# A two-weight FFT mixer: one product instruction a unit, negated weights on VectorE, odd row pair 6 in cosine and sine parts, and a new order list

## The chip, the cores and the metric

The kernel runs on one core of one Trainium2 chip. TensorE (PE) multiplies matrices into PSUM, VectorE (DVE) and ScalarE (ACT) read PSUM and SBUF, GpSimd (POOL) works on SBUF alone, and SyncE (SP) issues nearly all DMAs. The metric is the device time of one execution in microseconds. Three runs of the kernel before took 115.3, 115.53 and 116.19 us; the median, 115.53 us, is what the prediction is set against.

## The reference

`x` is 2048 x 1024 in bf16. Both branches A and B take the real 2-D FFT of the same `x`, multiply it by a complex weight of 2048 x 513, and transform back. A gate, one number for each row, mixes the two results.

```python
def ref(x, w_r, w_i):                       # A and B alike
    X = jnp.fft.rfft2(x.astype(jnp.float32), axes=(-2, -1))
    X = X * (w_r + 1j * w_i)
    return jnp.fft.irfft2(X, s=(S, D), axes=(-2, -1)).astype(jnp.bfloat16)

x = A_x
g = _sigmoid((x * gate_w).sum(-1, keepdims=True))
a = _A_ref(x, A_w_r, A_w_i)
b = _B_ref(x, B_w_r, B_w_i)
return g * a + (1 - g) * b
```

## The kernel before

**Transform by matrices.** The row index of 2048 is split as 128 x 16 and the column index is folded into four quarters, so that the whole transform becomes products with fixed cosine and sine matrices. Even and odd column frequencies are two halves of the work ("parity" 0 and 1). There are 16 units of rows, `n`: units 0 to 7 belong to parity 0, units 8 to 15 to parity 1.

**The order list.** The whole program is written as a list of short tokens in the string `ORDER` (lines 24 to 66). Each token calls one small function (table `fn`, line 665), in the order of the list. Every engine executes its own instructions strictly in that order, so the list is also the queue of each engine; buffers and PSUM banks come in rings, and an instruction waits until the earlier readers of its buffer are done. A letter names the engine that does a copy: A for ACT, D for DVE, P for POOL. The last figures of a PE token are PSUM banks. For instance `R:10:1:D` copies half 1 of unit 10 from PSUM on VectorE, and `J:10:0:6` computes unit 10 into banks 0, 1 and 6, 7.

The tokens in the order of the data:

- `x`, `c`, `W` load the input (nine DMAs), the constants and the 16 units of weights, all on SP. A unit of weights is 512 KB. Units 0 to 7 lie in the tile `ro`, 8 to 11 in `wx`, 12 to 15 in a part of `y` that has to be read out first.
- `F1` (line 331) multiplies one of 16 input slices with the first Fourier matrix, for the even (`e`) or odd (`o`) columns. `FC` copies one half of the result from PSUM, `FD` (two instructions, line 379) adds and subtracts it on DVE. For eight of the odd slices `FX` copies all of it on ACT and `FP` adds and subtracts on POOL.
- `neg` (line 278) writes minus the imaginary part of a constant, in two pieces of 128x256 and 128x768, into the tile `wn`.
- `F2` and `F3` (lines 455, 485) are the next two transforms of a unit; `T` and `X` copy their results from PSUM. There are two `T` and two `X` buffers.
- `P` (line 505, function `prod`) multiplies a unit's spectrum `X` with its weights on DVE. `P:n:0` and `P:n:1` do it in two instructions of 128x2048, for the real and the imaginary part of `X`. `P:n:b` does both in one instruction with broadcast operands. There are three `p` buffers. `Y`, `NA`, `N` repair one column of units 0 to 7.
- `J` (line 548, 32 matmuls in small tiles) starts the way back, `R` copies it from PSUM into `rl`, two halves a unit, and `H` stores each half (256 KB) to a scratch tensor in DRAM. The ring of `rl` has five buffers, which the output tiles use later too.
- `L:parity:v` loads one of eight row pairs `v` (512 KB) back from the scratch tensor with rows and columns exchanged. Parity 0 goes into `re`, parity 1 into `ro`. Loads of a parity wait for all 16 stores of it.
- `V` (line 576) applies the last transform over rows with the gate weights (`GH` to `GB` compute these), `VC` copies it, 8 matmuls of 128x128 each.
- The last transform over columns stands in two forms. `U` (line 592) does four matmuls of 128x512 which give the sum and the difference of the cosine and sine parts in PSUM. `C` (line 601) does four of 128x256 which give the two parts side by side; somebody then has to add and subtract them.
- For parity 0 all row pairs use `C`. `EX` copies the parts and two `EQ` combine them (DVE or POOL, line 626), or `ES` and `EF` do, or `E` copies the parts as they are.
- For parity 1, `OR` (line 646) adds or subtracts the even and the odd result on DVE straight from PSUM; `OC` and `OP` (line 642) do the same through an ACT copy and POOL. Row pair 3 goes another way: its even part is only copied (`E`), its odd part comes from `C`, `QD` (line 653) adds and subtracts the parts in fp32 on DVE, and `QP` (line 658) combines them on POOL.
- `S` stores a row pair to the output (512 KB, or 256 KB for a half).

**What sets the order around the change.** In DVE's queue the folds `FD` come first, then the 32 products with the small repairs, some `R`, `T`, `VC` copies and the gate weights `GA`, `GB` between them, then the even outputs and at last the odd ones.

Of the kernel before, what the change touches and what calls it, by code (L numbers as in the profile page):

```python
# [10 lines left out]
P = 128  # L11
S = 2048
D = 1024
# [11 lines left out]
warm:8 c:A:F1 x:S:0:1 x:S:1:1 c:A:gws x:S:2:2 tab:A F1:0:e:4 x:S:4:2 FC:0:e:D F1:1:e:7 F1:0:o:5 x:S:6:2 FC:1:e:A FD:0:e  # L25
FX:0:o:A F1:1:o:0 FD:1:e F1:2:e:6 x:S:8:2 FC:2:e:D FX:1:o:A F1:3:e:2 FD:2:e FC:3:e:A FD:3:e FP:1:o FP:0:o x:S:10:2 x:S:12:2
F1:2:o:4 F1:3:o:7 F1:4:e:0 F1:5:e:6 x:S:14:2 FX:2:o:A FP:2:o FC:4:e:D c:S:w0 c:S:WF:0:4 c:S:PM c:S:WF:4:16 c:S:EZ c:S:FD:0:1
W:S:0 W:S:1 c:S:E c:S:WJ:0:4 c:S:WJ:4:16 F1:7:e:1 FC:5:e:A W:S:2 FX:3:o:A FD:4:e FD:5:e FP:3:o F1:6:e:3 FC:7:e:A F1:5:o:4
F1:9:e:0 F1:8:e:6 F1:7:o:5 FC:6:e:A FX:5:o:A FC:9:e:A FD:7:e FD:6:e FC:8:e:A F1:11:e:1 gc:P F1:10:e:7 FX:7:o:A F1:4:o:4
F1:12:e:3 F1:13:e:2 FC:11:e:A FC:10:e:A FP:5:o FD:9:e FD:8:e FD:11:e FX:4:o:A F1:9:o:1 F1:15:e:6 F1:14:e:0 F1:11:o:5 FP:7:o  # L30
FC:12:e:A FC:13:e:A neg:A:0:4 FC:15:e:A FD:10:e FP:4:o FD:12:e FC:9:o:A F1:13:o:7 FC:14:e:A FD:13:e F1:12:o:4 F1:6:o:2
FD:15:e FD:14:e FD:9:o F2:1:0:6 FC:11:o:A neg:A:4:16 FC:13:o:A FX:6:o:A F2:1:1:3 T:1:0:A FD:13:o FC:12:o:A F1:15:o:2 T:1:1:A
FC:15:o:A FD:11:o F1:14:o:1 F1:10:o:0 F3:1:6 F2:0:0:3 F1:8:o:5 FD:12:o FC:10:o:A F2:0:1:4 FC:14:o:A FD:15:o FD:10:o F2:2:0:2
FD:14:o X:1:A FC:8:o:A T:0:0:A pw:P T:0:1:A T:2:0:A FD:8:o F2:3:0:0 F2:2:1:7 T:2:1:A F3:0:5 X:0:A P:1:1 P:1:0 P:0:1 F2:3:1:4
Y:1:3 F2:4:0:7 T:3:1:A FP:6:o F3:2:1 NA:1:D Y:0:5 W:S:9 NA:0:D W:S:3 W:S:7 P:0:0 W:S:8 W:S:11 N:1:D W:S:6 W:S:4 c:S:FD:1:2
W:S:5 c:S:IG T:4:0:A GH:6 X:2:A T:3:0:A GC:A Y:2:4 NA:2:D F2:5:1:1 P:2:0 P:2:1 W:S:10 F3:3:2 T:5:1:A F2:4:1:4 N:0:D GT:2:5
J:1:6:0 GT:0:5 X:3:A GT:1:5 GT:3:5 T:4:1:A F3:4:3 R:1:0:A F2:5:0:2 R:1:1:D X:4:A T:5:0:A GK:D J:0:6:0 F2:6:0:4 P:3:1 F2:6:1:5
Y:3:3 R:0:0:A F3:5:6 R:0:1:A P:3:0 NA:3:D GZ:0:2 F2:7:0:0 X:5:A F2:7:1:1 W:S:14 T:6:1:D T:6:0:D N:3:D N:2:D GS:0 P:4:0
T:7:0:D J:3:4:6 W:S:12 W:S:13 W:S:15 T:7:1:A GZ:1:0 R:3:1:A R:3:0:D J:2:6:2 Y:5:4 P:4:1 GS:1 Y:4:5 NA:5:D NA:4:D P:5:0 P:5:1
R:2:0:A N:4:D F3:7:0 R:2:1:A X:7:A F2:8:1:5 F3:6:6 F2:8:0:4 T:8:0:A T:8:1:D J:4:2:0 F3:8:4 H:0:0 H:1:0 X:6:A R:4:1:A Y:7:7  # L40
P:7:1 F2:9:0:6 N:5:D R:4:0:A Y:6:0 P:7:0 H:1:1 X:8:A NA:6:D T:9:0:A H:0:1 NA:7:D GA:D:4 F2:10:1:1 H:2:0 H:3:0 H:3:1 F2:9:1:0
P:6:0 T:9:1:A N:7:D P:6:1 T:10:1:A J:5:2:4 J:7:0:6 R:5:1:A R:5:0:A F2:10:0:5 H:4:0 F3:9:2 F2:11:0:4 P:8:1 H:2:1 R:7:0:A N:6:D
R:7:1:D J:6:0:6 GB:D:4 H:4:1 T:10:0:A X:9:A H:7:0 H:5:0 P:8:0 T:11:0:D R:6:0:A GA:D:0 R:6:1:A F2:11:1:2 F3:10:3 P:9:0 H:5:1
P:9:1 H:7:1 H:6:1 X:10:A H:6:0 J:8:0:6 T:11:1:A R:8:0:D R:8:1:A F2:12:0:4 H:8:0 T:12:0:A P:10:1 P:10:0 F3:11:2 F2:12:1:5
# [679 lines left out]
```

## Time and profile before

| what | value |
|---|---|
| median of three runs | 115.53 us |
| time of the profiled execution | 116.1 us |
| its span, first to last instruction | 114.3 us |
| granted TensorE clock, mean | 0.991 |
| PE busy | 103.0 us (90%) |
| DVE busy | 100.9 us (88%) |
| ACT busy | 86.4 us (76%) |
| POOL busy | 39.5 us (35%) |
| moved by DMA | 36.79 MB, 322 GB/s over the span |

The busy time of PE is that of pipelined matmuls whose ends are modelled. A row of the groups gives the line of the code, the engine, the operation, what it writes and reads, its shapes and count, and then the busy time together, the mean of one instruction in ns, and the idle time before it with what ended it. A row of the timeline gives start and length in us and how many instructions are merged in it; consecutive instructions of one engine overlap a little, so that two of 1.218 us can take 2.36 us together. In the chain of waits a row gives start, length and what was being waited for.

### The profile page before, as it was taken

The page shows a single profiled execution, that of the slowest core. Times are in us where ns is not written, and L with a number is a line of the kernel's source. Part 1 is how long each engine was busy: PE and PEld are TensorE (multiplying, and loading weights), DVE is VectorE, ACT ScalarE, POOL GpSimd, SP SyncE. Part 2 cuts the span into 40 slices and gives each one's busy share as a digit, 9 for nine tenths or more (in the row PEclk, how much of TensorE's full clock was granted, in tenths as well). Part 3 has the DMA queues.
Part 4 walks back from the last instruction along what each step waited for, and adds up shares of the span by engine and source line. Part 5 has one row for each costly group of instructions (what it writes and reads, how often), then busy time and mean ns, then how long its engine had stood idle before and what let it go on. Part 6 is the DMA issues. An engine that isn't in the chain of part 4 may idle for free.

```text
span 114.3 us, 3946 instructions
## 1 busy us (share of the span) xinstructions
PE 103.0 (90%) x1616; PEld 70.3 (61%) x1619; DVE 100.9 (88%) x175; ACT 86.4 (76%) x140; POOL 39.5 (35%) x61
## 2 busy tenths in 40 slices
PE   5969999999999988989898989998999999999930
PEld 2569999875546543534453547845998966566510
DVE  0068999999998999999999999999999598998990
ACT  4054989999799899999999999999689762325400
POOL 1019999800000000000000000830382999997300
PEclk9999999999999999999999999999999999999996
DMA  3999999999999899997969999996999998099655
GB/s 75 330 331 406 405 374 318 350 338 376 398 406 416 257 361 281 376 377 245 339 232 262 393 391 301 369 386 228 335 281 351 377 390 345 3 377 398 271 222 199
DMA packets 17794, 36.79 MB, mean 322 GB/s; under 512 B 1904, under 2 KB 10736, under 8 KB 17776
## 3 DMA queue, kind: packets, MB, share of 16 engines
q1 hardware_dynamic: 17488, 36.44, 88.4%
q8 instruction: 12, 0.20, 0.6%
q10 hardware_dynamic: 288, 0.10, 0.6%
q14 instruction: 6, 0.05, 0.1%
HBM read 23.96 MB, written 12.58 MB: 320 GB/s over the span
## 4 chain that ended last, share of the span: by engine, by line
PE 18%; DMA 10%; ACT 9%; DVE 6%; issue 3%; SPq 3%; DVEq 1%; ACTq 0%
PE ps L592 7%; DMA ro<-sc 7%; PE ps L576 5%; ACT rl L201 4%; DVE p L505 3%; PE ps L548 3%; DMA sc<-rl 3%; DVE ot L646 3%; SPq L565 3%; ACT T L201 2%; ACT X L201 1%; PE ps L485 1%; PE ps L455 1%; ACT V L201 1%; PE ps L601 1%
## 5 line engine op out<-in xcount | busy, mean ns | idle before, releaser
L626 POOL TENSOR_TENSOR re<-wx 128x256 f32<-128x256 f32 x15 | 12.9, 883 | 58.7 <-ACT wx L201 50.0
L201 ACT COPY wx<-ps 128x256 f32<-128x256 f32 (+1 forms) x41 | 18.0, 467 | 12.3 <-PE ps L592 5.7
L201 ACT CAST rl<-ps 128x1024 bf16<-128x1024 f32 x25 | 24.6, 1042 | 0.7 <-PE ps L548 0.7
L548 PE MATMUL ps<-p,wj 32*64 32x512 bf16 x512 | 19.6, 380 | 2.6 <-ACT rl L201 1.4
L505 DVE TENSOR_TENSOR p<-X,ro 128x2048 bf16<-128x2048 bf16 x16 | 19.1, 1218 | 0.0
L455 PE MATMUL ps<-fd,y 128*128 128x256 bf16 x128 | 17.7, 273 | 0.4 <-ACT rl L201 0.2
L201 ACT CAST V<-ps 128x512 bf16<-128x512 f32 x23 | 13.0, 593 | 6.3 <-PE ps L576 4.8
L201 ACT CAST X<-ps 128x1024 bf16<-128x1024 f32 x16 | 16.7, 1044 | 0.2 <-PE ps L485 0.2
L331 PE MATMUL ps<-f,re 128*128 128x128 bf16 x256 | 15.9, 225 | 0.9 <-DMA re<-in_x_dram 0.9
L331 PEld LDWEIGHTS <-re 128*128 128x128 bf16 x256 | 15.4, 101 | 1.9 <-DMA re<-in_x_dram 1.4
L379 DVE TENSOR_TENSOR y<-ps,wx 128x256 bf16<-128x256 f32 x48 | 16.3, 416 | 0.1
L201 ACT CAST T<-ps 128x512 bf16<-128x512 f32 x26 | 15.2, 628 | 0.8 <-PE ps L485 0.8
L646 DVE TENSOR_TENSOR ot<-re,ps 128x512 bf16<-128x512 f32 x22 | 13.9, 683 | 0.9 <-PE ps L592 0.5
L548 PEld LDWEIGHTS <-wj 32*64 32x64 bf16 x512 | 8.2, 103 | 10.4 <-issue 6.8
L455 PEld LDWEIGHTS <-y 128*128 128x128 bf16 x128 | 11.1, 97 | 5.0 <-issue 3.8
L379 POOL TENSOR_TENSOR y<-wx 128x256 bf16<-128x256 f32 x16 | 11.1, 731 | 7.3 <-ACT wx L201 7.3
L592 PE MATMUL ps<-ig,V 128*128 128x512 bf16 x53 | 13.2, 379 | 0.2
L485 PE MATMUL ps<-T,wf 64*64 64x512 bf16 (+1 forms) x128 | 10.4, 334 | 0.6 <-ACT T L201 0.3
L505 DVE TENSOR_TENSOR p<-X,y 128x2048 bf16<-128x2048 bf16 x8 | 9.9, 1282 | 0.0
L601 PE MATMUL ps<-ig,V 128*128 128x256 bf16 x72 | 9.8, 273 | 0.0
L505 DVE TENSOR_TENSOR p<-X,wx 128x2048 bf16<-128x2048 bf16 x8 | 9.5, 1218 | 0.0
L203 DVE COPY wx<-ps 128x256 f32<-128x256 f32 (+1 forms) x8 | 4.2, 549 | 5.9 <-PE ps L331 5.9
(61 smaller groups left out, 144.3 us busy)
## 6 DMA issues: line engine op xcount, KB each, us to landing
sc<-rl SPq DMA_DIRECT2D x32, 256.0 KB, 5.5
ro<-in_we_dram SPq DMA_DIRECT2D x8, 512.0 KB, 6.9
re<-sc SPq DMA_DIRECT2D x8, 512.0 KB, 7.1
ro<-sc SPq DMA_DIRECT2D x8, 512.0 KB, 6.3
re<-in_x_dram SPq DMA_DIRECT2D x7, 512.0 KB, 9.0
out_dram<-ot SPq DMA_DIRECT2D x7, 512.0 KB, 2.7
wx<-in_wo_dram SPq DMA_DIRECT2D x4, 512.0 KB, 7.2
y<-in_wo_dram SPq DMA_DIRECT2D x4, 512.0 KB, 6.6
```

What stands on the lines that cost most here:

```text
L201: nc.scalar.copy(out=out, in_=in_)
L331: nc.tensor.matmul(o, lhsT=lh, rhs=rh, start=(h == 0), stop=(h == 1))
L379: Q[e].tensor_tensor(yo[:, v, k:k + n, s1, :], a.rearrange("p (k c) -> p k c", c=4), b.rearrange("p (k c) -> p k c", c=4), op)
L455: nc.tensor.matmul(ps[:, v * 256:v * 256 + 256], lhsT=y[:, v, par, b, 2 * t:2 * t + 2, :, :].rearrange("p j s c -> p (j s c)"), rhs=C["FD" ...
L485: nc.tensor.matmul(view(ps[ho, tt * 512:(tt + 1) * 512], dst), lhsT=lh, rhs=view(T[hp(jh), tt, :], src), start=(w == 0), stop=(w == 1))
L505: nc.vector.tensor_tensor(p[:, int(r)], xb, w, ALU.mult)
L548: nc.tensor.matmul(o, lhsT=lh, rhs=src[r, ri, wi, tt], start=(q == 0), stop=(q == 3))
L576: nc.tensor.matmul(ps[:, ch * 128:ch * 128 + 128], lhsT=RR[par][:, v, ch // 2, s, c0 + 256 * ab:c0 + 256 * ab + 128], rhs=Ew[:, s1, :], st ...
L592: nc.tensor.matmul(ps, lhsT=Vs[par, v][:, s, ch, :], rhs=rh, start=(ch == 0), stop=(ch == 3))
L601: nc.tensor.matmul(ps[:, o:o + 256], lhsT=Vs[par, v][:, s, ch, :], rhs=g[:, o:o + 256], start=(ch % 2 == 0), stop=(ch % 2 == 1))
L626: Q[e].tensor_tensor(EV[:, v, s, 256 * h:256 * h + 256], t[:, 0], t[:, 1], (ALU.add, ALU.subtract)[h])
L646: nc.vector.tensor_tensor(otile(v)[:, s, h, :], EV[:, v, s], PS["O", 1, v, s], (ALU.add, ALU.subtract)[h])
```

## The change

Four things change, all of them in the order list; no function is altered.

1. The 32 tokens `P:n:0` and `P:n:1` become 16 tokens `P:n:b`.
2. `neg:A:0:4` and `neg:A:4:16` become `neg:D:0:4` and `neg:D:4:16`.
3. Row pair 6 is done as row pair 3: `U:1:6:s` becomes `C:1:6:s`, the even part is copied by `E:6:s` instead of `EX:6:s` and four `EQ:6`, and four `OR:6` become four `QD:6` on DVE and four `QP:6` on POOL.
4. The list is ordered anew throughout, with other engines for some copies and other PSUM banks.

Copies that change engine, counted over the whole list: `R` on DVE from 7 to 8, `VC` on DVE from 9 to 5, `FC` on DVE from 3 to 2, `EX` on DVE from 4 to 2 and `E` on DVE from 0 to 2; `EQ` on POOL from 15 to 11, on DVE 5 in both; `T` on DVE 6 in both.

The core of the diff, the stretches that the prediction speaks of:

```diff
-FX:0:o:A F1:1:o:0 FD:1:e F1:2:e:6 x:S:8:2 FC:2:e:D FX:1:o:A F1:3:e:2 FD:2:e FC:3:e:A FD:3:e FP:1:o FP:0:o x:S:10:2 x:S:12:2
...
-FC:12:e:A FC:13:e:A neg:A:0:4 FC:15:e:A FD:10:e FP:4:o FD:12:e FC:9:o:A F1:13:o:7 FC:14:e:A FD:13:e F1:12:o:4 F1:6:o:2
...
-P:15:0 P:15:1 GA:D:8 J:13:4:2 EX:0:1:A VC:0:2:0:A VC:0:2:1:A J:14:0:6 R:13:0:A R:13:1:A J:15:4:2 GB:D:8 R:14:0:D EQ:0:1:1:D
-GA:D:12 H:13:0 R:14:1:A R:15:0:A GB:D:12 R:15:1:A H:14:1 H:14:0 H:13:1 C:0:1:0:6 H:15:0 H:15:1 L:0:5 L:1:3 L:1:1 V:0:4:1:7
...
-U:1:6:1:6 V:1:7:0:4 U:1:6:0:0 VC:1:7:0:A OR:7:1:1 OR:7:1:0 OR:6:1:0 U:1:7:0:4 OR:6:1:1 OR:6:0:1 OR:6:0:0 OR:7:0:1 OR:7:0:0
-S:S:7:1 S:S:6 S:S:7:0
+warm:8 c:A:F1 x:S:0:1 x:S:1:1 c:A:gws x:S:2:2 F1:0:o:1 F1:1:o:4 F1:0:e:2 FC:0:e:D F1:1:e:3 tab:A FX:0:o:A FX:1:o:A x:S:4:2
+x:S:6:2 x:S:8:2 F1:3:e:6 F1:2:e:1 FP:0:o c:S:EZ x:S:10:2 FC:3:e:A c:S:w0 c:S:E x:S:12:2 x:S:14:2 gc:P FP:1:o FC:1:e:D FD:1:e
...
+F2:1:1:2 F2:0:0:3 neg:D:4:16 FD:10:o FD:15:o neg:D:0:4 FD:12:o T:1:0:A FP:5:o F1:14:o:7 T:1:1:A F2:0:1:5 F1:11:o:6 FD:8:o
...
+R:6:1:A GA:D:8 R:6:0:D H:5:1 H:4:0 H:7:1 H:7:0 H:6:0 H:6:1 W:S:13 F2:12:0:3 X:10:A F2:11:1:7 F2:12:1:0 T:11:0:A W:S:12
...
+L:0:6 L:0:7 L:0:4 L:0:5 V:0:0:1:2 F2:15:1:3 R:10:0:A F3:14:0 R:10:1:A VC:0:0:1:A J:11:4:6 X:14:A F2:15:0:0 R:11:1:A C:0:0:1:1
+H:8:1 P:12:b H:8:0 H:9:1 H:9:0 H:10:0 H:10:1 V:0:0:0:6 R:11:0:A T:15:1:D GB:D:4 T:15:0:D P:14:b F3:13:2 V:0:1:1:7 EX:0:1:A
...
+EX:2:1:D GB:D:12 EQ:2:1:0:D R:13:1:D VC:0:1:0:A C:0:2:0:5 EX:2:0:A H:12:1 H:12:0 J:15:0:6 H:11:0 H:11:1 R:15:1:A V:0:6:0:4
+V:0:6:1:5 H:14:0 R:15:0:A H:14:1 C:0:1:0:3 H:13:0 H:13:1 GB:D:8 EX:1:0:A VC:0:6:0:A EQ:1:1:1:D EQ:2:0:0:D H:15:1 V:0:4:1:6
...
+VC:1:4:1:D S:S:3 U:1:7:0:4 U:1:4:0:3 U:1:7:1:5 U:1:4:1:7 OR:7:0:0 OR:7:0:1 OC:4:0:A S:S:0 S:S:5 S:S:2 EQ:7:1:1:P OR:7:1:0
+OR:7:1:1 OR:4:1:0 OR:4:1:1 S:S:6 S:S:7:0 OP:4:0:1 OP:4:0:0 S:S:7:1 S:S:4
```

65 lines of the change are left out of this document (30 added, 35 removed).

## The prediction

> **What bounds the kernel now.** I read the slices of the page first, to see which engine is ever free, then the stretches, then the chain of waits.
>
> ```profile
> span 114.3 us, 3946 instructions
> ...
> PE   5969999999999988989898989998999999999930
> ...
> DVE  0068999999998999999999999999999598998990
> ACT  4054989999799899999999999999689762325400
> ```
>
> PE and DVE are full from the fourth slice to the end, ACT to about 80 us; only the ends and the last third of ACT have room. The stretches say which engine has no slack in which part (columns: busy us and instructions of PE, weight loads, DVE, ACT, POOL; clock; DMA share; GB/s).
>
> ```profile
> 11.20:24.40 13.20, 13.20 (x213) 12.29 (x211) 13.16 (x41) 12.50 (x31) 10.97 (x27) 1.00 1.00 357
> 24.40:77.70 53.30, 49.20 (x968) 28.11 (x967) 52.31 (x69) 51.53 (x71) 3.25 (x2) 1.00 0.97 343
> 88.40:109.70 21.30, 20.99 (x197) 13.87 (x198) 19.06 (x34) 9.34 (x18) 17.79 (x18) 1.00 0.80 313
> ```
>
> From 11.2 to 24.4 us DVE does the folds, without a hole (13.16 of 13.20). From 24.4 to 77.7 us, first to last product, it is busy 52.31 of 53.30: its instruction list sets the pace. From 88.4 us on it is PE, 20.99 of 21.30. What lies between the last product and 88.4 is in the chain of waits, with the tail after it:
>
> ```profile
> 77.83 0.90 PE ps L548 x24
> ...
> 78.75 1.93 ACT rl L201 x2
> ...
> 81.04 3.23 DMA sc<-rl
> ...
> 95.54 0.62 PE ps L576 x8
> 96.16 2.59 PE ps L592 x12
> 98.75 0.45 PE ps L576 x8
> ...
> 107.56 2.54 DVE ot L646 x4
> ```
>
> ```profile
> L576 PEld LDWEIGHTS <-ro x72: 95/98/98, 88.6 to 95.9; 128*128 128x128 bf16 x72
> L565 SPq DMA_DIRECT2D ro<-sc x8: 332/434/1352, 84.5 to 88.6; - x8
> ...
> DMA to landing us min/median/max: 4.0/6.3/10.1
> ```
>
> The last unit's matmuls end at 78.73, its two copies at 80.68, the last store is issued at 81.04 and lands 3.23 us later; the eight loads of parity 1 start at 84.5, the quickest takes 4.0 us, so 88.5, and PE's first use of `ro` is at 88.6. From there PE's work decides (V, U, C), then DVE's last `OR`, then the last output store. So the time is: folds, DVE's product stage, a fixed trip through DRAM, PE's odd stage, a tail.
>
> **The change, part by part.** The sum is made against the profiled span of 114.3 us, whose execution took 116.1 us; that execution is 0.57 us above the median of 115.53, so I add the difference to the median. I counted tokens of DVE's queue in both lists.
>
> ```profile
> L505 DVE TENSOR_TENSOR p<-X,ro 128x2048 bf16<-128x2048 bf16 x16 | 19.1, 1218 | 0.0
> L203 DVE CAST rl<-ps 128x1024 bf16<-128x1024 f32 x7 | 8.5, 1221 | 0.3
> L203 DVE CAST V<-ps 128x512 bf16<-128x512 f32 x9 | 6.1, 682 | 0.2 <-PE ps L601 0.2
> L442 DVE TENSOR_TENSOR ea<-ea,e 128x512 bf16<-128x512 bf16 x4 | 1.7, 416 | 0.0
> L278 ACT ACTIVATE wn<-wf 128x768 bf16<-128x768 bf16 x1 | 0.9, 857 | 0.0
> ...
> 29.70 2.36 DVE L505 TENSOR_TENSOR p<-X,ro 128x2048 bf16<-128x2048 bf16 x2
> ...
> 70.67 4.02 DVE L505 TENSOR_TENSOR p<-X,y 128x2048 bf16<-128x2048 bf16 x3
> 72.02 3.25 POOL L626 TENSOR_TENSOR re<-wx 128x256 f32<-128x256 f32 x2 [49.69 <-ACT wx L201]
> ```
>
> *Products.* Two of 1.218 us take 2.36 us together: the second starts 1.14 us after the first, so about 0.08 us of each is hidden by its neighbour. A line through 128x512 (0.416) and 128x2048 (1.218) has a slope of 0.522 ns an element and 0.149 us fixed. One instruction of 4096 elements is then 2.29 us, against 2.36: 0.07 us saved a unit, 1.1 us in 16. Ends: nothing saved, and the whole fixed part, 16 x 0.149 = 2.4. I take 1.1, as the pair of row 29.70 shows it directly. [...]
>
> *Negations.* DVE has no such row before. The same line gives 0.55 us for 768 elements and 0.28 for 256; less 0.08 overlap each, +0.67 us. Bounds 0.2 (two very short DVE instructions) and 0.83 (no overlap). I keep 0.67, since the 128x512 row is near. They stand before the last folds, so all products move. ACT loses 0.857 us and its smaller piece, which buys nothing while DVE sets the pace. [...]
>
> *Start of the folds.* DVE's rows around the first input DMAs:
>
> ```profile
> 9.00 0.42 DVE L203 COPY wx<-ps 128x256 f32<-128x256 f32 x1 [1.33 <-PE ps L331]
> 9.46 1.42 DVE L379 TENSOR_TENSOR y<-ps,wx 128x256 bf16<-128x256 f32 x4
> ...
> 11.24 13.01 DVE L379 TENSOR_TENSOR y<-ps,wx 128x256 bf16<-128x256 f32 x39
> ```
>
> The new list does the odd groups of slices 0 and 1 first, so the first even copy comes two PE groups later. But before, DVE stands idle 1.33 us ahead of 9.00 us, until the third input DMA has fed PE. The late start falls into that hole, and the removed copy on DVE (0.42) is work taken from the same place, so 20 folds of 0.667 (13.01 x 2 / 39) remain from about 11.2 us in both. The three small constants now ahead of the last two input DMAs, and copies that ACT takes over, come late by my reading at slices 14 and 15: +0.2 us (0 to 0.5).
>
> *Product stage.* Between the first and last product DVE gets one `R` more (+1.14, row of 1221 less overlap), two `GA` more (2 x 0.41 = +0.82) and two `VC` fewer (2 x 0.60 = -1.20). `T`, `NA`, `N`, `GB` are as many as before. With the products: -0.34. Before, one product ran beside two POOL additions: rows 70.67 and 72.02 show three products in 4.02 us instead of 3.50, and two additions in 3.25. In the new list one POOL addition (`EQ:0:1:0`) falls into the stage, so I leave that loss of 0.5 us as it is. The last product then ends 0.67 + 0.2 - 0.34 = +0.53 us later.
>
> *Last product to first odd load.* The last two products before:
>
> ```profile
> 75.21 2.35 DVE L505 TENSOR_TENSOR p<-X,y 128x2048 bf16<-128x2048 bf16 x2
> ```
>
> `J:15` now uses bank 0, which holds `C:0:2:1` until DVE's `EX:2:1` has copied it, and that stands behind the last product: 0.60 (a copy of 128x512 like `VC`), then some 1.2 us of matmuls and 1.93 of copies. Before, the last copy ended 3.1 us after the last product (80.68 against 77.56) and SP issued 0.36 later, being busy with the other stores; the new order frees it. Sum 3.7 + 0.05 against 3.48: +0.27. The trip itself stays: one load of parity 0 precedes the odd ones in both lists.
>
> *Odd stage on PE.* Two `U` become two `C`.
>
> ```profile
> 103.98 0.86 PE ps L592 x4
> ...
> 71.76 0.44 PE ps L601 x4
> ```
>
> 2 x (0.86 - 0.44) = -0.84. PE begins with row pairs 1, 3, 6, 0 in the order of their loads, as before with 3, 1, 0; I see no new wait.
>
> *Tail.* DVE has as many instructions for odd rows as before (22 `OR` + 4 `QD` against 18 + 8). POOL gains 4 `QP` and loses 4 `EQ`.
>
> ```profile
> 104.94 6.35 DVE L646 TENSOR_TENSOR ot<-re,ps 128x512 bf16<-128x512 f32 x10 [0.35 <-issue]
> 107.75 1.89 PE L592 MATMUL ps<-ig,V 128*128 128x512 bf16 x8
> 100.58 2.50 POOL L642 TENSOR_TENSOR ot<-re,wx 128x512 bf16<-128x512 f32 x2
> 103.03 0.73 POOL L626 TENSOR_TENSOR re<-wx 128x256 f32<-128x256 f32 x1
> ...
> out_dram<-ot SPq DMA_DIRECT2D x7, 512.0 KB, 2.7
> ...
> out_dram<-ot SPq DMA_DIRECT2D x2, 256.0 KB, 2.4
> ```
>
> Now DVE ends 111.29 - 109.64 = 1.65 us after PE. In the new list POOL does 6 `OP` + 8 `QP` of 1.25 and `EQ:7:1:1` of 0.73 from the first odd `OC` on, 18.2 us. PE reaches that after three `V` (0.45), a `C` and a `U`, 2.65 us into the odd stage; with a copy of 0.6 POOL begins at 3.3 and ends at 21.5, and `OR:7:1` waits for `EQ:7:1:1` at 19.0. Four `OR` of 0.63 follow: 21.5. PE ends at 21.0 - 0.84 = 20.2, so DVE and POOL end at least 1.3 us after it; since POOL will hardly run without a hole I take 1.85, +0.2 (bounds -0.3 and +0.5). The last store is 512 KB instead of 256 KB: +0.3.
>
> **Sum:** +0.53 + 0.27 - 0.84 + 0.2 + 0.3 = **+0.46 us**, span 114.8, and 115.53 + 0.46 = **116.0 us**.
>
> **The rivals.**
>
> *A, faster.* The merged products save the whole fixed part (2.4 instead of 1.1) and the negations cost 0.2 instead of 0.67: 1.3 + 0.47 = 1.8 less, **114.2 us**. For it: the rows of short instructions do show a fixed part of 0.149. Against it: the pair of 2.36 us. [...]
>
> *B, slower: the stores wait behind the loads.* SP before, around the loads of parity 0 (`re<-sc`):
>
> ```profile
> 60.54 3.47 SPq L565 DMA_DIRECT2D re<-sc x7
> 64.45 17.04 SPq L560 DMA_DIRECT2D sc<-rl x14
> ```
>
> In the new list seven loads of parity 0 stand ahead of all stores of units 8 to 12 on SP, and two weight loads ahead of those; before, unit 8's stores and all weights had gone. Two stores and two weight loads are 1.5 MB at the 343 GB/s of the stretch: 4.4 us more in front of unit 11's stores. The copy of unit 15 needs unit 10's buffer, that of unit 14 unit 8's. By my count these land about 2 us ahead; the weight loads fit into the hole while the first load of parity 0 waits for its stores. If that hole is not there, up to 4.4 - 2 = 2.4 us come onto the path: **117.9 us** with half of it to all, 117.2 to 118.4.
>
> *C, slower: the product stage gets holes.* A product of 2.29 us gives nothing to `J` until it is done, and releases `X` and lets the next `R` on DVE start later; ACT (51.53 of 53.30) and PE (49.20) have so little slack that a hole of 0.15 us for each of 16 units gives +2.4: **118.4 us**. Against: `J` needs both halves already now.
>
> *D:* the broadcast over four dimensions falls to a lower rate; at the rate of the PSUM copies (0.682 us for 512 elements, less 0.149 fixed) a product would take 4.4 us, 16 x 2.0 more than a pair: **148 us**. `X` is read with a broadcast dimension in the rows before already, so there is hardly a chance.
>
> **How the numbers follow.** About 1% is what a measurement of this kernel can tell from no change. The forecast, within 1% (114.4 to 116.7): 0.43. A: 0.22. B: 0.19, C: 0.14, D: 0.02; together 0.35 slower. The unknown costs (products -1.3 to +1.1, negations -0.5 to +0.2, tail -0.5 to +0.5) span 114.3 to 117.3; the range reaches to A and B and into C, **113.9 to 118.2**.
>
> **What would show it.** Products of 2.25 to 2.35 us each in the groups, the last ending near 78.1; negations of 0.3 and 0.55; first use of `ro` near 89.4; 48 `U` matmuls instead of 56 and 80 `C` instead of 72; from there to PE's end 20.2 us; POOL nearly gapless in its last 18 us. It would be wrong if DVE has more than 1 us of holes in the product stage (C), if `R` on ACT waits for a landing store near 75 us (B), or if the first product starts later than 25.6 us.

## The result, and the profile after

The changed kernel takes **115.08 us** (median of 20 runs, 114.09 to 117.04) beside 115.91 us of the kernel before (20 runs, 115.14 to 117.14), 0.83 us less. The ratio is **0.9893**, 95% interval 0.9866 to 0.9921; here and below a ratio leaves out the slow runs, those more than 1.5% above the fastest of their kernel (the medians are then 114.65 and 115.89 us), while a median is that of all runs. So the change is worth about 1%, which is small but clear of the noise. I had forecast 116.0 us and 0.46 us slower; the time lies in my range, on the other side of no change. Single runs scatter by 2 to 3 us in both kernels, so each experiment below is compared with the runs of the kernel before that belong to it.

The profiled execution after has a span of 113.6 us and took 115.38 us. From its page, the slices of the span:

```profile
span 113.6 us, 3933 instructions
...
PE   5999979999988879798998989979999699999910
...
DVE  0079989999998999999999999999559849999870
ACT  4267848999989999999999999999976565635200
```

The stretches of after (columns as in the prediction: PE, weight loads, DVE, ACT, POOL, clock, DMA share, GB/s), from the first to the last product, from there to the first odd `V`, and from there to PE's end:

```profile
24.40:76.10 51.70, 46.35 (x947) 28.15 (x945) 51.12 (x54) 50.43 (x69) 2.50 (x1) 1.00 0.94 337
76.10:87.40 11.30, 11.19 (x165) 9.41 (x165) 8.64 (x18) 9.75 (x19) 4.88 (x7) 1.00 0.85 283
87.40:107.80 20.40, 19.37 (x192) 13.52 (x196) 17.74 (x32) 10.18 (x19) 17.24 (x16) 1.00 0.77 300
```

The product stage is 51.6 us long where it was 53.05, and DVE is still full in it. Between the stages PE is full (11.19 of 11.30), and in the odd stage PE now has a full us without work. The chain of waits of after, around the last store and the first odd loads (start, length, what was waited for):

```profile
66.73 8.73 DMA sc<-rl
75.46 0.03 ACTq L200
75.49 0.66 ACT rl L200
...
76.19 0.61 PE ps L575 x8
76.79 0.44 PE ps L600 x4
77.23 1.05 PE ps L547 x32
...
79.21 1.03 ACT rl L200
...
80.25 3.42 DMA sc<-rl
83.67 0.02 issue
...
84.26 5.43 DMA ro<-sc
89.69 0.05 issue
89.74 0.28 PE ps L575 x2
```

The chain goes through the landing of a store at 75.46, which ended a wait in ACT's queue ahead of a copy `R`, and of the last store at 83.67 (84.28 before), and then not through the first odd load but through the second, which PE gets at 89.7. The groups and the timeline show the parts of the change:

```profile
L501 DVE TENSOR_TENSOR p<-X,ro 128x4096 bf16<-128x4096 bf16 x8 | 18.1, 2279 | 0.0
```

```profile
19.73 0.66 DVE L279 TENSOR_SCALAR wn<-wf 128x768 bf16<-128x768 bf16 x1
...
21.64 0.21 DVE L279 TENSOR_SCALAR wn<-wf 128x256 bf16<-128x256 bf16 x1
...
24.43 2.27 DVE L501 TENSOR_TENSOR p<-X,ro 128x4096 bf16<-128x4096 bf16 x1
```

A product is 2.28 us, the negations are 0.66 and 0.21 us, and the first product starts at 24.43 us, where it started at 24.51 before.

The numbers of this table are used below for every kernel. They are taken from the same trace records as the views (landings from the completions of the DMAs). "Last load ahead" is the last of the loads of parity 0 that stand in front of the closing row of stores on SP; the number in brackets is how many stores land after it. "PE's end" is the end of PE's last weight load, in every kernel 0.49 us ahead of the end of its last matmul, which the prediction used (109.64 before, 108.30 after).

```
kernel                    last product  last store  last load   last store  from load to   first odd  PE's
                          ends          issued      ahead lands lands       store (stores) V          end
before                    77.56         81.05       74.08       84.28       10.20 (14)     88.56      109.15
before, second profile    78.24         81.72       75.34       85.12        9.78 (14)     89.24      110.15
after                     76.03         80.26       72.71       83.67       10.96 (16)     87.36      107.81
after, second profile     76.23         80.35       72.59       83.57       10.98 (16)     87.39      108.66
merge in before           79.44         82.93       75.59       86.29       10.70 (14)     90.47      111.13
split in after            77.23         80.98       72.71       83.65       10.94 (16)     87.95      107.81
order alone               77.47         81.21       72.65       83.78       11.13 (16)     88.27      108.69
additions early in after  77.02         80.77       72.51       83.48       10.97 (16)     87.64      107.68
additions late in before  76.77         80.42       74.28       83.88        9.60 (14)     88.09      108.86
weights early in after    76.54         81.28       73.74       84.70       10.96 (16)     88.33      108.84
one load less ahead       76.40         80.52       70.31       82.85       12.54 (16)     91.29      110.78
one load more ahead       75.98         80.48       72.92       83.84       10.92 (16)     87.49      106.89
```

### The profile page after: what moved, and what is told of

Its sections match the earlier page's. It is cut to its first block, busy times and chain, and to the rows that moved or that the text cites. A ratio compares the mean times of both kernels' runs of the same rounds, so it can differ in the third digit from the quotient of the medians.

```text
span 113.6 us, 3933 instructions
## 1 busy us (share of the span) xinstructions
PE 99.9 (88%) x1616; PEld 69.7 (61%) x1619; DVE 97.7 (86%) x157; ACT 87.1 (77%) x142; POOL 41.0 (36%) x61
## 4 chain that ended last, share of the span: by engine, by line
DMA 43%; PE 36%; DVE 5%; issue 4%; ACT 4%; SPq 3%; DVEq 1%; ACTq 0%
DMA sc<-rl 17%; DMA re<-in_x_dram 12%; PE ps L591 8%; PE ps L575 6%; PE ps L454 6%; DMA re<-sc 5%; DMA ro<-sc 5%; PE ps L330 4%; PE ps L547 4%; DMA y<-in_wo_dram 3%; ACT rl L200 3%; PE ps L484 3%; PE ps L600 2%; PE ps L403 2%; SPq L559 2%
## 5 line engine op out<-in xcount | busy, mean ns | idle before, releaser
L625 POOL TENSOR_TENSOR re<-wx 128x256 f32<-128x256 f32 x11 | 9.5, 888 | 60.2 <-DMA re<-sc 48.4
L200 ACT CAST V<-ps 128x512 bf16<-128x512 f32 x27 | 15.7, 613 | 7.8 <-PE ps L575 5.1
L501 DVE TENSOR_TENSOR p<-X,ro 128x4096 bf16<-128x4096 bf16 x8 | 18.1, 2279 | 0.0
L547 PE MATMUL ps<-p,wj 32*64 32x512 bf16 x512 | 17.1, 380 | 0.9 <-ACT V L200 0.4
L645 DVE TENSOR_TENSOR ot<-re,ps 128x512 bf16<-128x512 f32 x18 | 11.3, 682 | 0.6 <-POOL re L625 0.5
L591 PE MATMUL ps<-ig,V 128*128 128x512 bf16 x45 | 11.5, 379 | 0.2
L600 PE MATMUL ps<-ig,V 128*128 128x256 bf16 x80 | 11.2, 272 | 0.2 <-ACT rl L200 0.2
L202 DVE CAST rl<-ps 128x1024 bf16<-128x1024 f32 x8 | 9.7, 1218 | 0.4 <-PE ps L547 0.4
L657 POOL TENSOR_TENSOR ot<-pq 128x512 bf16<-128x512 f32 x8 | 9.9, 1276 | 0.0
L575 PEld LDWEIGHTS <-ro 128*128 128x128 bf16 x128 | 7.8, 98 | 2.9 <-DMA ro<-sc 1.4
```

The costliest lines, as they stand in the source:

```text
L200: nc.scalar.copy(out=out, in_=in_)
L501: nc.vector.tensor_tensor(p[:], xb, wb, ALU.mult)
L547: nc.tensor.matmul(o, lhsT=lh, rhs=src[r, ri, wi, tt], start=(q == 0), stop=(q == 3))
L575: nc.tensor.matmul(ps[:, ch * 128:ch * 128 + 128], lhsT=RR[par][:, v, ch // 2, s, c0 + 256 * ab:c0 + 256 * ab + 128], rhs=Ew[:, s1, :], st ...
L591: nc.tensor.matmul(ps, lhsT=Vs[par, v][:, s, ch, :], rhs=rh, start=(ch == 0), stop=(ch == 3))
L600: nc.tensor.matmul(ps[:, o:o + 256], lhsT=Vs[par, v][:, s, ch, :], rhs=g[:, o:o + 256], start=(ch % 2 == 0), stop=(ch % 2 == 1))
```

## The experiments

The kernels below ran in four groups, each beside the kernel before, whose medians there were 116.25 (29 runs), 116.02 (17), 116.40 (29) and 116.23 us (19). In the second group (row pair 6 as before with its additions earlier, order alone, weights early) one run of the kernel before came out at 113.95 us, 1.2 us ahead of the next, and the ratios of that group lean on it; they are given, but I go by the medians there.

**Both kernels again.** No edit.

> The changed kernel itself once more, as the reference of this group. Measured before: 0.989 of the kernel before (115.1 us). Theory 'order' (the new head removes a hole in DVE's folds): the first product starts again at 24.4 us of the span, within 0.3. Rival 'scatter' (the input DMAs landed early by chance in the one profile): the first product starts anywhere from 24 to 25.5 us, and the landing of the third input DMA moves with it.

115.61 us (12 runs) beside 116.25: ratio 0.9944, interval 0.9903 to 0.9986. The gain is there a second time, smaller: 0.64 us. In its profile the first product starts at 24.42 us, as in the first, with the third input DMA at 6.64 us instead of 6.39.

> The kernel before once more, for its profile alone. Theory 'scatter': its third input DMA, which landed at 8.3 us of the span in the profile that the prediction used and at 6.1 to 7.1 us in four later ones, lands near 6.5 us; the first product then starts near 24.0 us instead of 24.5, as in the run with merged products in the old order. Rival 'order': it lands near 8.3 us again, since the list itself makes it late, and the first product starts at 24.5.

One run, 117.11 us with its profile (span 115.3 us). Its use is the head of the kernel. In the profile that the prediction was made from, DVE had no hole from 11.2 to 24.4 us. The same stretch of this second profile, and its timeline:

```profile
11.20:24.40 13.20, 12.66 (x195) 11.24 (x193) 12.51 (x39) 11.31 (x29) 11.05 (x27) 1.00 0.96 361
```

```profile
7.95 0.42 DVE L203 COPY wx<-ps 128x256 f32<-128x256 f32 x1 [0.29 <-PE ps L331]
16.95 7.44 DVE L379 TENSOR_TENSOR y<-ps,wx 128x256 bf16<-128x256 f32 x22 [0.69 <-ACT wx L201]
```

Here the third input DMA landed at 6.59 us and not at 8.30, the early hole is 0.29 us and not 1.33, and DVE then waits 0.69 us for ACT: the first product starts at 24.30. Two kernels further down have the same list up to the first product (merged in the old order, additions held back in the kernel before). There DVE's holes between 11.2 us and the first product are 0.60 and 0.10 us, and the product starts at 24.01 and 23.73. So in the old order the start scatters by 0.8 us, the 24.51 against which I priced the change is the latest of four, and that DVE was full ahead of it does not show that DVE sets the pace there.

**Merged products in the old order.**

```diff
-... P:1:1 P:1:0 ... P:15:0 P:15:1 ...
+... P:1:b ... P:15:b ...
```

Each unit's `P:n:b` stands at the place of the second of the two tokens in the list of before.

> The kernel before with one product instruction a unit, at the place of the second of the two; nothing else. Theory 'DVE sets the pace of the product stage': 16 x 0.07 = 1.1 us less, 114.8 us, ratio 0.990. With the whole fixed part of 0.149 us a unit saved: 113.5 us, 0.979. Rival 'the other engines have no slack either' (ACT, PE): the saving turns into holes on DVE, 115.9 us, 1.00. The profile then shows idle time on DVE between 24 and 77 us of 1.5 us and more instead of 1.0.

118.07 us: slower by 1.8 us, ratio 1.0173 (1.0128 to 1.0218). Neither side of what I had written reached above 115.9 us. The products themselves are cheaper: start to start they cost DVE 35.95 us in place of 37.17. But DVE's holes in the product stage grow from 1.0 to 4.3 us. Its waits there, from the view of waits of this kernel for DVE between 24 and 80 us:

```profile
DVE rl L202 <- PE ps L547: 1.2, 1, 1.2
DVE rl L202 <- ACT rl L200: 0.9, 1, 0.9
DVE rl L202 <- DMA sc<-rl: 0.9, 1, 0.9
DVE np L524 <- PE ps L516: 0.7, 1, 0.7
DVE np L524 <- PE ps L484: 0.5, 1, 0.5
```

This is rival C of the prediction, in the order for which the rival was not written: where a half product stood behind something that had to come first, the whole one now waits, or what follows it does.

**Products split again in the new order.**

```diff
-... P:1:b ... P:15:b ...
+... P:1:1 P:1:0 ... P:15:1 P:15:0 ...
```

> The changed kernel with two product instructions a unit, side by side. Theory 'DVE sets the pace': 1.1 us more than the changed kernel, 116.2 us, ratio 1.00; the product stage grows from 51.6 to 52.7 us. Rival 'loads decide the odd stage': the product stage grows, but the later stages absorb it and the time is 115.1 to 115.5 us, 0.990 to 0.995.

115.52 us (12 runs), where the changed kernel itself took 115.61 beside the same runs of before; the ratios are 0.9974 (0.9932 to 1.0016) and 0.9944 (0.9903 to 0.9986), and their intervals overlap. So merging gives nothing that can be measured in the new order, although the products cost DVE 36.45 us in place of 35.37, just the 1.08 us that I had counted (1.1), and the last product ends 1.2 us later (77.23). From its chain of waits:

```profile
80.97 2.68 DMA sc<-rl
```

The last store is issued 0.7 us later than in the changed kernel and lands at the same time, 83.65 against 83.67. The 1.1 us is saved on DVE and lost again in front of that landing.

**Order alone.** The new order with split products, negations on ACT and row pair 6 as before.

```diff
-... neg:D:4:16 ... P:1:b ... E:6:0:A ... C:1:6:1:0 ... QD:6:1:0 ...
+... neg:A:4:16 ... P:1:1 P:1:0 ... EX:6:0:A ... U:1:6:1:0 ... OR:6:1:0 ...
```

> The new order with the three named parts taken back: two product instructions a unit side by side, negations on ACT, row pair 6 as in the kernel before. Theory 'the order is the gain': 0.990 to 0.997 of the kernel before, about as the changed kernel. Rival 'the parts are the gain': 1.1 (products) + 0.8 (pair 6) - 0.7 (negations) = 1.2 us slower than the changed kernel, ratio 1.000 to 1.005.

116.62 us (6 runs) beside 116.02: 0.6 us slower than before, ratio 1.019 (1.010 to 1.028). The new order is no gain by itself.

**Row pair 6 as before, in the new order** (products merged, negations on DVE).

```diff
-... E:6:0:A ... E:6:1:D ... C:1:6:1:0 ... QD:6:1:0 ... QP:6:0:0:P ...
+... EX:6:0:A ... EX:6:1:D ... EQ:6:0:0:P ... U:1:6:1:0 ... OR:6:1:0 ...
```

> The changed kernel with row pair 6 as in the kernel before (U instead of C, EX and four EQ on POOL instead of E, four OR instead of QD and QP). PE gets 0.84 us more in the odd stage, POOL 2.1 us less in the tail. Theory 'PE's work sets the odd stage': 0.8 us more than the changed kernel, 115.9 us, ratio 0.996 to 1.00. Rival 'loads and POOL set it': the time moves by less than 0.3 us, or falls by up to 0.5 us because POOL's last chain is shorter.

In this version the four POOL additions of row pair 6 came so late that the buffers they read had been used again, so that the even part of row pair 6 is not the reference's. 117.1 us, ratio 1.0052 (1.0005 to 1.0100). The place of the additions is changed with the part, so it says little on the part itself.

> The changed kernel with row pair 6 as in the kernel before, its four EQ now on POOL before the first odd row pair. PE gets 0.84 us more in the odd stage, POOL 2.1 us less in the tail. Theory 'PE's work sets the odd stage': 0.8 us more than the changed kernel (ratio to it 1.007). Rival 'loads and POOL set it': within 0.3 us of the changed kernel.

With the additions earlier, 115.75 us (6 runs) beside 116.02; the ratio is 1.0104 (1.0021 to 1.0186). Six measurements of kernels that do row pair 6 in parts in the new order (after twice, split, and the three further below with the negations on ACT, the additions early, and one load more ahead) are 0.6 to 1.3 us under their runs of before by the medians; this one is 0.3 under and order alone 0.6 over. Two more kernels with row pair 6 in parts, which change what stands in the queue of SP (weights early, one load less ahead), are 0.1 and 0.5 over.

**Weights early.**

```diff
-... W:S:15 ... W:S:13 ... W:S:12 ...
+... W:S:15 W:S:13 W:S:12 ...
```

> The changed kernel with the last two weight loads (units 12 and 13, 1 MB) issued right behind those of units 14 and 15, before the stores, instead of just ahead of the loads of parity 0. Theory 'the DMA queue decides when the odd loads start' (in the changed kernel the 16 stores of units 8 to 15 landed 0.69 us apart without a hole up to the last): the queue in front of the last store is shorter by up to 2.5 us, the last store lands 0.4 to 1.2 us earlier, and the time falls by 0.4 to 1.0 us. Rival 'DVE's products decide': the last store lands within 0.2 us of the changed kernel's, and so does the time.

116.14 us beside 116.02, ratio 1.0091 (0.9993 to 1.0190): nothing gained, and a miss for both sides. The two weight loads now stand in front of the last even stores, which land 1.66 us later (59.68 against 58.02), the loads of parity 0 start later, and the last odd store lands at 84.70 instead of 83.67.

**Negations on ACT in the new order.**

```diff
-... neg:D:4:16 ... neg:D:0:4 ...
+... neg:A:4:16 ... neg:A:0:4 ...
```

> The changed kernel with the two negations back on ScalarE, at their place in the new list. My prediction put +0.67 us on the path for them. If that holds, VectorE's list before the first product gets 0.87 us of work shorter, the first product starts near 23.7 us instead of 24.4, and the run is about 0.6 us faster than the changed kernel. Rival, which I now hold for likelier: at this point ScalarE with its copies of T and X sets the start of the first product, VectorE has room, and 0.7 to 1.1 us of negations in front of ScalarE's copies make the first product start at the same time or up to 0.6 us later (24.4 to 25.0); the run is then the same to 0.6 us slower than the changed kernel.

115.14 us, ratio 0.991 (0.9873 to 0.9948): as the changed kernel. DVE's timeline ahead of the first product:

```profile
19.66 2.73 DVE L378 TENSOR_TENSOR y<-ps,wx 128x256 bf16<-128x256 f32 x8
23.19 1.42 DVE L378 TENSOR_TENSOR y<-ps,wx 128x256 bf16<-128x256 f32 x4 [0.81 <-ACT wx L200]
24.53 2.28 DVE L501 TENSOR_TENSOR p<-X,ro 128x4096 bf16<-128x4096 bf16 x1
```

DVE has 0.87 us less to do and waits 0.81 us for ACT, on which the negations now stand: the first product starts at 24.53 instead of 24.43. Order alone, which has them on ACT too, waits 1.27 us there and starts at 24.89; with the negations on DVE this order starts at 24.41 to 24.70 us (25.31 in the kernel with other PSUM banks). My +0.67 us for the negations falls; the rival holds.

**POOL additions held back, in the kernel before.**

```diff
-... EQ:0:0:0:P ... EQ:1:1:0:P ... EQ:2:0:0:P ...
+... EX:2:0:D EQ:2:0:0:P EQ:0:0:0:P EQ:1:1:0:P ...
```

> The kernel before, with the two POOL additions that ran beside a product held back: POOL's first three additions are re-ordered so that the first one waits for a copy that stands behind the last product. Theory: in the kernel before a product shared time with these additions and took 1.75 us instead of 1.22; then every product takes 1.22, the product stage gets 0.5 to 0.6 us shorter (53.0 to 53.9 before), and the run is about 0.5 us faster, unless the later POOL work is late for the odd stage. Rival: the long product was chance or has another cause; one product is again 0.5 us longer than the others, or the stage keeps 53.0 to 53.9 us, and the run is within 0.2 us of before.

The timelines of DVE and of POOL:

```profile
70.41 3.49 DVE L505 TENSOR_TENSOR p<-X,y 128x2048 bf16<-128x2048 bf16 x3
```

```profile
81.42 3.33 POOL L626 TENSOR_TENSOR re<-wx 128x256 f32<-128x256 f32 x4 [59.58 <-DMA sc<-rl]
```

The same three products took 4.02 us in the kernel before, beside additions; now 3.49, and all products cost 36.56 us instead of 37.17. The cause of the long product is shown. But the time is 116.09 beside 116.40, ratio 1.0004 (0.9962 to 1.0045): the 0.6 us does not arrive. Already the product stage keeps its 53.04 us, since DVE's holes in it are 1.59 us instead of 0.99. What the last product gained (76.77 instead of 77.56) came from an early first product (23.73), and half of that is lost at the landing: the stores behind the loads of parity 0 land without a gap here (9.60 us for 14).

**POOL additions early, in the changed kernel.**

```diff
-... EQ:0:1:0:P ... EX:0:0:A ...
+... EQ:0:1:0:P EQ:0:1:1:P ... EX:0:0:A EQ:0:0:0:P EQ:0:0:1:P ...
```

> The changed kernel with three more POOL additions right behind the one that falls into the product stage, so that four of them want to run beside the last products. Theory (additions and products take time from each other, as in the kernel before): two products get 0.5 us longer each or one gets 1 us longer, the stage is 52.1 to 52.7 us instead of 51.6 to 51.8, and the run 0.5 to 1 us slower. Rival (beside a long product the addition is the one that waits, as the single one of 2.5 us in the changed kernel): the additions take over 2 us each, products keep 2.28 us, the stage stays within 0.2 us of 51.7, and the run within 0.3 us of the changed kernel.

DVE, POOL and the chain of waits:

```profile
71.93 5.10 DVE L501 TENSOR_TENSOR p<-X,y 128x4096 bf16<-128x4096 bf16 x2
```

```profile
73.19 4.42 POOL L625 TENSOR_TENSOR re<-wx 128x256 f32<-128x256 f32 x2 [1.05 <-ACT wx L200]
```

```profile
80.76 2.72 DMA sc<-rl
```

Both sides pay: two products take 5.10 us in place of 4.48 and two additions 4.42 in place of 1.4. The last product ends 1.0 us later. The stage, 52.6 us, is what the theory had said, and the time, 115.29 us with a ratio of 0.9914 (0.9873 to 0.9955), is what the rival had said: as the changed kernel. Both had hung the time on the stage; the last store lands at 83.48, 0.2 us earlier than there.

**Unit 15 in other PSUM banks.**

```diff
-... C:0:2:1:0 ... V:0:1:0:4 P:15:b EX:2:1:D ... R:13:1:D VC:0:1:0:A C:0:2:0:5 EX:2:0:A ... J:15:0:6 ... R:15:0:A ...
+... C:0:2:1:3 ... V:0:1:0:1 VC:0:1:0:A P:15:b R:13:1:D J:15:0:4 EX:2:1:D ... C:0:2:0:5 ... R:15:0:A EX:2:0:A ...
```

> The changed kernel with the matmuls of the last unit freed from a VectorE copy that stands behind the last product: they use another PSUM bank and stand first on TensorE after the last product, and the copy of unit 13 on VectorE comes first after it. Theory: the way from the last product to the issue of the last store is 3.4 to 3.8 us instead of 4.1 to 4.2, all later steps follow, and the run is 0.4 to 0.6 us faster than the changed kernel (about 114.6 where that one has 115.1). Rival: the store of unit 15 waits for the stores ahead of it on SP or for a buffer that a landing store sets free; the issue of the last store stays 4.0 us or more behind the last product and the run within 0.2 us of the changed kernel.

This edit was a mistake of mine: `J` takes four banks, not two, so its matmuls stood behind another copy on ACT instead (0.99 us of wait), and row pair 2's even part is overwritten before it is copied, so that it is not the reference's. 117.63 us; the last store is issued 5.2 us after the last product. It decides nothing.

**One load less, and one more, ahead of the last stores.** In the changed kernel seven loads of parity 0 stand ahead of the last sixteen stores on SP and one behind them.

```diff
-... L:0:6 L:0:7 L:0:4 L:0:5 ... H:15:0 ... L:0:3 L:1:1 ...
+... L:0:6 L:0:4 L:0:5 ... H:15:0 ... L:0:7 L:0:3 L:1:1 ...
```

> The changed kernel with the load of row pair 7 of parity 0 taken out of the seven loads that stand ahead of the last sixteen stores on SP, and put behind the last store, beside the load of row pair 3. VectorE, ScalarE and TensorE keep their lists up to the last store. Theory (the DMA queue sets when the last store lands: in the changed kernel it lands 10.96 us after the last of these loads, sixteen stores at 0.68 us without a gap): with 1.27 us less in front, the last store lands 0.8 to 1.3 us earlier, at 82.4 to 82.9 us instead of 83.6 to 83.7, while the last product still ends at 76.0 to 76.3. Rival (the end of the product stage sets it, through the matmuls and copies of unit 15 and a trip of fixed length): the last store lands at 83.4 to 83.8 as before. The time itself says little here: the even work of row pair 7 now waits for its load, which both theories put at 1 to 3 us more.

The queue of SP (start of the issue, length, how many):

```profile
78.86 2.02 SPq L559 DMA_DIRECT2D sc<-rl  x3
80.93 0.98 SPq L564 DMA_DIRECT2D re<-sc  x2
83.05 4.05 SPq L564 DMA_DIRECT2D ro<-sc  x8
```

The granted clock of this profile is 1.00 up to 83 us and 0.81 from there to 92 us, so the landing of the last store is not touched by it. The odd loads are issued 0.2 us after the last store has landed: at 83.05, where it was 83.88. The last store was issued at 80.52 and landed at 82.85, 2.33 us later instead of 3.4, with the last product at 76.40. The queue theory said 82.4 to 82.9, the other 83.4 to 83.8. The time, 116.75 us, has the wait of row pair 7 in it.

```diff
-... L:0:4 L:0:5 ... H:15:0 ... L:0:3 L:1:1 ...
+... L:0:4 L:0:5 L:0:3 ... H:15:0 ... L:1:1 ...
```

> The changed kernel with the load of row pair 3 of parity 0 taken from behind the last store and put ahead of the last sixteen stores, as an eighth load in front of them. Theory (the DMA queue sets it): all stores land 1.25 us later, the last one at 84.7 to 85.1 us, the first odd load lands 0.8 to 1.2 us later than 87.3, and the run is 0.4 to 1 us slower than the changed kernel. Rival (the end of the product stage sets it): the last store lands at 83.5 to 83.8, the load of row pair 3 no longer stands between it and the odd loads, and the run is the same or up to 0.3 us faster.

```profile
78.72 2.12 SPq L559 DMA_DIRECT2D sc<-rl  x3
84.05 3.72 SPq L564 DMA_DIRECT2D ro<-sc  x8
```

A miss for the queue theory as I had put it: the last store lands at 83.84 and not at 84.7 or later, and the time is 115.23 beside 116.23 (ratio 0.9932, 0.9893 to 0.9970), as the changed kernel. The eight loads land at 72.92, only 0.2 us after the seven of the changed kernel, because a gap of 1.1 us between two of them there (2.41 us from one landing to the next, where 1.25 to 1.3 is usual) is not there here. From the last load to the last store it is 10.92 us again. The landing, within 0.1 us, and the time are what the rival had said, so this run alone does not tell the two apart; the one with a load less does, and so do the two in which the last product ends 1.0 and 1.2 us later (additions early, products split) and the last store lands as in the changed kernel.

## Why the prediction was wrong, point by point

**The first product (+0.87 in my sum; measured -0.08).** The step that failed is "They stand before the last folds, so all products move", with "which buys nothing while DVE sets the pace". The sign of the forecast hung on it: without the 0.67 us for the negations my sum is -0.21 us. With them on ACT the gain is the same (115.14 us beside 116.40), since ACT then makes DVE wait for 0.81 us; put on DVE, they fill that hole. The -0.08 is between single profiles; against the mean of the four starts of the old order (24.14 us) the two profiles of after start 0.3 us later, and which part makes that, the +0.2 for the later small constants or another, is open. That the durations (0.66 and 0.21 us against 0.55 and 0.28) came out near was luck. The piece of 128x768 took 0.35 us where no POOL addition ran beside it (additions early), 0.44 to 0.66 us beside one in most kernels, and 1.05 (products split) and 1.38 us (unit 15 in other banks) where it ended only after two of them.

**The product stage (-0.34; measured -1.45, from 53.05 to 51.60; 53.94 to 51.81 in the second profiles).** Here the step is "so I leave that loss of 0.5 us as it is". The terms that I worked out came as said: one product instead of two saves 1.08 us in 16 (1.1), `R`, `GA` and `VC` as counted. But the single addition cost DVE nothing. From POOL's and DVE's timelines of after:

```profile
68.58 2.50 POOL L625 TENSOR_TENSOR re<-wx 128x256 f32<-128x256 f32 x1 [48.40 <-DMA re<-sc]
```

```profile
68.21 2.28 DVE L501 TENSOR_TENSOR p<-X,y 128x4096 bf16<-128x4096 bf16 x1
70.41 1.22 DVE L202 CAST rl<-ps 128x1024 bf16<-128x1024 f32 x1
```

The addition starts inside the product and ends 0.59 us after it, 2.50 us in place of 0.73; the product keeps 2.28 us, and what follows on DVE is a copy from PSUM, which loses nothing either (1.22 us). Where a second product follows, the products can take longer, as in the kernel before (4.02 us for three, 3.49 with the additions held back) and with the additions early (5.10 for two, 4.48 in after). They need not: with the products split again, an addition that starts 0.03 us into a product ends 0.59 us after the next one, and neither product loses anything.

```profile
69.24 2.91 POOL L626 TENSOR_TENSOR re<-wx 128x256 f32<-128x256 f32 x1 [48.79 <-DMA re<-sc]
```

```profile
69.21 2.35 DVE L505 TENSOR_TENSOR p<-X,y 128x2048 bf16<-128x2048 bf16 x2
```

The addition is 0.6 to 0.7 us of DVE's time; the rest of the difference is fewer holes (0.58 us instead of 0.99; 1.82 in the second profile of before). Where the additions were held back in the kernel before, the same 0.6 us went into holes, so it takes both to shorten the stage. The rows of 2.50, 2.91, 4.02 and 5.10 us show that of products and additions side by side one or the other took longer, and the row of 1.22 us that a copy from PSUM did not; what makes one of them wait for the other is not shown. The 1.08 us saved by the merging is 0.07 us for each of the 16 instructions saved.

**From the last product to the first odd load (+0.27; "The trip itself stays").** This is the step whose failure matters most for how such a kernel is read. The way to the issue became 0.74 us longer (4.23 against 3.49), more than the 0.27 that I gave. The matmuls of unit 15 start 1.13 us after the last product, where I had 0.60, and the copy that I named is not what holds them: `EX:2:1` ends at 76.67 us, but ahead of them PE has a `V` and a `C` (76.19 to 77.23 in the chain of after), and that `V` had waited 0.32 us for `R` on ACT.

The longer way costs nothing, since the trip is not fixed: from its issue to its landing the last store takes between 2.33 and 3.47 us in the kernels of the table. In the seven profiles of the table that have the new order with seven loads ahead, or eight, the last store lands 10.92 to 11.13 us after the last of those loads, at 0.68 us for each of the sixteen, and it does so whether the last product ends at 76.0 or at 77.5. Taking one load away brought the landing forward by 0.8 us, though the last product ended 0.4 us later. So two chains end there nearly together, the queue of stores and the product stage. With the 2.33 us from issue to landing of that run, an estimate for after by the products alone is 82.6 us, and the queue makes it 83.67.

In the kernel before the fourteen stores take 10.20 us where 0.68 each makes 9.6, and the 0.6 us stands in the intervals between the last five landings (0.80, 0.72, 0.78 and 1.06 us). The first of these ends with a store that landed 2.20 us after its issue, as quickly as any of these stores, and it was issued 0.80 us after the one ahead of it, which took 2.20 us too; so I take it that nothing stood ahead of it in the queue and the product stage was behind. The last three were issued 0.4 to 0.6 us apart, and why they landed further apart than 0.68 us is open. In the new order these gaps are gone, and that is what arrives at the landing of the 1.5 us of products (84.28 to 83.67). The queue is also why splitting the products again moved nothing at the landing (83.65).

**The odd stage on PE (-0.84).** PE's work fell as I had said, but in both profiles of after the time does not show it. From the first odd `V` to PE's end it is 20.59, 20.91, 20.66, 20.77 us in the four profiles of the old order and 20.42 with order alone; it is 19.86 (products split), 20.04 (additions early) and 19.40 us (one load more ahead) with row pair 6 in parts: means of 20.67 and 19.77, 0.9 us less. (With the negations on ACT and the weights early, where the second odd load is late by 0.6 and 1.2 us, it is 20.29 and 20.51.) In the two profiles of after it is 20.45 and 21.27, and the weight loads of after show what takes it back:

```profile
87.36 0.90 PEld L575 LDWEIGHTS <-ro 128*128 128x128 bf16 x16 [0.29 <-DMA ro<-sc]
89.73 0.45 PEld L575 LDWEIGHTS <-ro 128*128 128x128 bf16 x8 [1.15 <-DMA ro<-sc]
```

"I see no new wait" failed: PE waits 1.15 us (1.97 in the second profile of after) for the second odd load, which lands 2.4 and 3.2 us behind the first, where 1.25 to 1.4 is usual, and 18.1 us after that landing PE ends in both. In the kernels with 19.4 to 20.04 that load is on time (no such row for the second load with one load more ahead):

```profile
87.49 0.90 PEld L575 LDWEIGHTS <-ro 128*128 128x128 bf16 x16 [0.38 <-DMA ro<-sc]
```

The best comparison is the kernel that differs from the changed one in row pair 6 alone (as before, additions earlier), since it has nearly the same wait:

```profile
87.10 0.90 PEld L575 LDWEIGHTS <-ro 128*128 128x128 bf16 x16
89.45 0.45 PEld L575 LDWEIGHTS <-ro 128*128 128x128 bf16 x8 [1.12 <-DMA ro<-sc]
```

Its stage is 21.42 us. Less PE's waits for odd loads, the stage is 19.2 to 19.5 us in every profile with row pair 6 in parts and 20.1 to 20.4 us in every other one. So the 0.84 us of work is shown; whether it reaches the medians is not, since in the profiles the stage of after is 0.14 us shorter and 0.36 us longer than that of before.

What delays the second load is open. In the trace a 16 KB instruction load starts within 0.1 us of the issue of the first odd load in after twice and with the weights early, and 0.6 to 1.0 us behind it, or with one load more ahead 1.5 us in front of it, where the second load is on time. With row pair 6 as before it starts 0.5 us behind it, and the second load is late all the same. No run was made to show that the one causes the other.

**The tail (+0.2 and +0.3).** DVE ends 2.22 us after PE (2.15 before; by the end of the last matmul, as in the prediction, 1.73 and 1.66), so +0.07; the last store of 512 KB takes 0.55 us more from DVE's end to the end of the span (3.57 against 3.02) where I gave 0.3.

Together, profile against profile: -1.53 at the last product, +0.74 to the issue, +0.18 to the landing, -0.59 to the first odd `V` (the load of parity 0 that stands in between takes 1.25 us instead of 1.82), -0.14, +0.07, +0.55: -0.72, the difference of the spans. The second profiles give -2.0, +0.6, -0.2, -0.3, +0.4, +0.1 and +0.5. My sum had +0.53, +0.27, 0, 0, -0.84, +0.2 and +0.3. The sign went wrong in the first two of its steps, the head and the product stage, which I put 2.1 us too late; 0.6 us of what I had missed arrives at the landing.

**The rivals.** A (114.2 us, by a larger saving of the products) gave the right side for the wrong reason: the saving was my own 1.1 us and is not what made the kernel faster. B (stores behind loads) had the right place, the queue on SP, and its sign shows a little: `R` on ACT waits for a landing store near 75 us, in after without idle time (ACT's copies start 0.9 us apart there), with one load more ahead for 0.3 us and with the negations on ACT for 0.4 us. Its 2.4 us did not come; the queue only bounds the gain. C (holes) did not come in the new order, and did come, at 1.8 us, when the products were merged in the old one. D did not come.

What stays open: how much of the gain belongs to row pair 6, the negations, the merging and the order. Taken back alone in the changed kernel, the merging and the place of the negations make no difference that could be measured. But row pair 6 as before (115.42 to 116.13 us) and order alone (116.28 to 117.25 us) differ in just these two, ran in one group, and their six runs each do not overlap: 0.9 us between the medians. Either the two together are worth what neither is alone, or something else sets these two kernels apart; no run tells which.

## What to carry to other kernels

A stage that is full in one profile need not set the pace: look at a second profile before an edit is priced there, since the holes can differ from one to the next (here 0.04 us of them on DVE with the third input DMA at 8.30 us, 0.69 with it at 6.59), and since the start of a stage can scatter by more than the edit is worth (here 0.8 us). Where an engine's last instruction is followed by a trip through DRAM, ask whether the store lands at its own latency or behind a queue; if the stores land at an even spacing (here 0.68 us), the end is counted from the transfers ahead of them, and time saved on the engine stays there (here a last product 1.2 us earlier left the landing where it was, 83.67 against 83.65 us). And two instructions made one save what the trace's own pair shows (here 0.07 us a unit), but they must stand where both halves could have started: the same edit was worth nothing in one order and cost 1.8 us in another.

## What I had not expected of the hardware

- 256 KB stores to DRAM landed one every 0.68 us, sixteen in 10.92 to 10.98 us in six of the seven profiles of the table with the new order and seven or eight loads ahead, while the last product ended anywhere from 75.98 to 77.23 us; 512 KB loads back from DRAM landed mostly 1.12 to 1.48 us apart in the profiles of before and after, with longer intervals at changing places (1.60 to 2.65 us in before, 2.37 to 2.89 in after).
- In the changed kernel the last store behind that queue landed 3.42 us after its issue; with one load less ahead it took 2.33 us, and the quickest of the last stores in the kernel before took 2.20.
- A POOL addition of 0.73 us took 2.50 us beside a product without costing DVE anything. With a second product behind the first, the products took 0.53 us longer in the kernel before and 0.62 us with the additions early, and nothing longer beside an addition of 2.91 us with the products split; a copy from PSUM behind the product kept its 1.22 us.
- Merging two VectorE instructions saved 0.07 us a unit, half of the fixed part of 0.149 us that the prediction's rows of 128x512 and 128x2048 give.
